# Weight pieces and expert pieces handled two at a time, and a new hand-written order for the first tiles

## The chip, the cores and the metric

The kernel runs on one core of one Trainium2 chip. The metric is the device time of one execution in microseconds (us), the median of several runs. The profile is of one such execution, taken by the hardware profiler.

## The reference, cut to what matters

Three stages follow one another. The first is a gated linear attention over 4 batches, 8 heads, 768 steps and head size 48; the second a feed-forward layer with a leaky ReLU; the third gives each token to one of 8 experts, at most 384 tokens to each.

```python
for t in range(S):                       # attention, f = sigmoid(f_logit)
    state = f[:, :, t, :, None] * state + einsum('bhd,bhde', k[:, :, t], v[:, :, t])
    y[:, :, t] = einsum('bhd,bhde->bhe', q[:, :, t], state)
x = y as [3072, 384]
h = x @ w_in                             # 384 -> 2048
x = maximum(0.01 * h, h) @ w_out         # 2048 -> 384
...                                      # token -> expert by the order of the logits, 384 tokens per expert
out[mask] = maximum(x[mask] @ w1[e], 0) @ w2[e]      # 8 experts, 384 -> 1024 -> 384
```

## The kernel before, in words

The 3072 tokens are 24 tiles of 128. Attention goes tile by tile in chunks; a tile takes the steps `f` (decay: exponentials and a sum on TensorE into `P`), `p` (the scaled `ks` and `qs`), `k` (transposed keys `kT`, copied to `kp`), `a` (scores `A`, masked into `am`), `y` (output, and the state's update `U`) and `x` (a DMA transpose of the result `ys` into `xT`). Three tiles make a group; group g then goes through the second stage's first product (`first`, 16 row blocks f of 128 hidden columns, 9 matmuls of 384 columns into `hp` for each block) and second product (`second`, `xp`). All products run as high and low float16 halves, three matmuls for one.

The weights come as float64 bit patterns in pairs of int32. A piece of `w_in` (one block f of 128 columns) is loaded, put together into float32 by three VectorE instructions (`as_f32`: `winu`), copied to its high half by ScalarE (`winh`) and its low half made by VectorE (`winl`); `w_out` likewise (`woutu`, `wo`). `first` and `second` take a block only after its piece has been emitted (`ready`). The first eight pieces of `w_in` land in tiles of the later `gh` and `gl` buffers (`win_e`), the rest in a ring with the tag `ws` (`win_s`, `wout_s`, `xw_s`).

The expert weights (`w1`, `w2`) are read from HBM in 64 pieces of 128x768 float32, split into a high half by ScalarE (`expert_high`) and a low half by VectorE (`expert_low`), and written back to HBM (`w1d`, `w2d`), from which the third stage fetches one expert's rows. This stream runs beside the second stage, one piece for every 21 large matmuls emitted.

A `Driver` with a clock of its own, advanced by the emitted large matmuls, decides when attention, weight pieces and stream are emitted; each engine executes its own queue in order. For the first tiles the order is written by hand: `START` is the list of steps (a letter, a tile or piece, one part each) and `LOADS` that of the loads on SP's queue; a load waits there behind those ahead of it. Every recorded operation carries line 85, so tile names tell them apart.

Of the kernel before, what the change touches and what calls it, by code (L numbers as in the profile page):

```python
# [9 lines left out]
F32 = mybir.dt.float32  # L10
# [51 lines left out]


LOADS = """
f:0 f:1 qk:0 f:2 v:0 f:3 qk:1 v:1 qk:2 f:4 w:0 f:5 qk:3 w:1 v:2 w:2 qk:4 x:0 v:3 qk:5 x:1 x:2 w:3 w:4 w:5 w:6 w:7 v:4 w:8 w:9 v:5 w:10
"""
START = """
z7 f0 f1 f0 f1 p0 f2 f3 p1 p0 a0 p1 a0 f2 k0 a0 f3 a1 k0 a1 y0 k1 a1 p2 p2 p3 y0 y0 w0 k2 k1 p3 a2 k2 a2 y1 y0 w1 a2 f4 y1 y1 y1 f4 p4 w2 k3 a3 k3 a3
p4 y2 a4 w1 f5 f5 a3 x0 y2 y2 w0 w2 a4 y2 y3 w1 x1 p5 a4 y3 p5 a5 w0 w2 a5 k4 y3 x2 k4 a5 w3
"""  # L70


# [20 lines left out]
def body(tc, qk, v, f_logit, w_in, w_out, w_gate, w1, w2, out):  # L93
# [6 lines left out]
    Dm = H * D  # L100
# [6 lines left out]
    GW = 384  # L107
    RT = 3
    NWD = 0
    WU = 4  # L110
    LEAD, PACE0, W0, FT, PB = 3, 1300.0, 1000.0, 8, 3

    with ExitStack() as ctx:
# [49 lines left out]
                XT[name, n] = t  # L163

        qkT = [apool.tile([128, 2, NP, 128], F32, name=f"qkT{i}") for i in range(3)]
        NPC = 16
        WIC = FF // NPC
        FPC = NF // NPC
        w_in_s, w_out_s, w_in_n = {}, {}, set()

        def load_win(i):
            if i in w_in_n:
                return
            w_in_n.add(i)
            if i < 8:
                if i % 4 == 0:
                    w_in_s["early"] = gpool.tile([128, 4, KT, WIC, 2], I32, name="win_e", tag=("gh", "gl")[i // 4])
                t = w_in_s["early"][:, i % 4]
            else:
                t = aw.tile([128, KT, WIC, 2], I32, name="win_s", tag="ws", bufs=3)  # L180
            SP.dma_start(t, ap(w_in, i * WIC * 2, [[2 * FF, 128], [256 * FF, KT], [2, WIC], [1, 2]]))
            w_in_s[i] = t

        def load_wout(i):
            t = aw.tile([128, FPC, Dm, 2], I32, name="wout_s", tag="ws", bufs=3)
            SP.dma_start(t, ap(w_out, i * FPC * 256 * Dm, [[2 * Dm, 128], [256 * Dm, FPC], [2, Dm], [1, 2]]))
            w_out_s[i] = t


# [71 lines left out]
            return u.bitcast(F32)  # L261

        def split_win(i):
            s = slice(i * WIC, (i + 1) * WIC)
            r = as_f32(w_in_s.pop(i), "win")
            yield
            copy(winh[:, :, s], r, SWI)
            yield
            DVE.scalar_tensor_tensor(winl[:, :, s], r, SWI, winh[:, :, s], op0=OP.mult, op1=OP.subtract)
# [3 lines left out]

        def split_wout(i):
            r = as_f32(w_out_s.pop(i), "wout")
            s = slice(i * FPC, (i + 1) * FPC)
            copy(wo[:, s, 0], r, SWO)
            DVE.scalar_tensor_tensor(wo[:, s, 1], r, SWO, wo[:, s, 0], op0=OP.mult, op1=OP.subtract)

# [63 lines left out]

        def load_expert(src, dst, scale, e, i):

            t = aw.tile([128, XW], F32, name="xw_s", tag="ws", bufs=3)
            x = SP.dma_start(t, src[e * 128:(e + 1) * 128, i * XW:(i + 1) * XW])
            if turned_at:
                behind(x, turned_at[-1])
            xw_s.append(t)  # L350

        def expert_high(src, dst, scale, e, i):
            x = xw_s.pop(0)
            o = aw.tile([128, XW], F16, name="xw_h", tag="wu", bufs=WU)
            z = copy(o, x, scale)
            if fed:
                behind(z, fed[-1][0])
            xw_o.append((dst[e * 128:(e + 1) * 128, 2 * i * XW:2 * (i + 1) * XW], x, scale, o))

        def expert_low():  # L360
            to, x, scale, h = xw_o.pop(0)
            o = aw.tile([128, XW], F16, name="xw_l", tag="wsc", bufs=WU)
            z = DVE.scalar_tensor_tensor(o, x, scale, h, op0=OP.mult, op1=OP.subtract)
            if fed:
                behind(z, fed[-1][1])
            return (to[:, :XW], h), (to[:, XW:], o)

        def expert_weights():
            ps = list(expert_pieces())
            for p in ps[:2]:  # L370
                load_expert(*p)

            n0 = big[0]
            for n in range(len(ps) + 1):
                while big[0] < n0 + n * PX:
                    yield 100.0
                if n < len(ps):
                    expert_high(*ps[n])
# [158 lines left out]
        def first(gi, nn, gx):  # L537
            xh, xl = gx[:, :KT], gx[:, KT:]
            N = 128 * nn
            gp = g2pool[0] if gi == LAST else gpool  # L540
            gh = gp.tile([128, NF, GW], F16, name="gh")
            gl = gp.tile([128, NF, GW], F16, name="gl")
            gh_[gi], gl_[gi] = gh, gl
            for f in range(NF):
                while ("in", f * NPC // NF) not in ready:
                    yield None
                fs = slice(128 * f, 128 * (f + 1))
                hp = psum.tile([128, GW], F32, name="hp", tag="mm", bufs=3)[:, :N]
                for c in range(KT):
                    mm(hp, winh[:, c, fs], xh[:, c, :N], c == 0, False)  # L550
                    yield N / 2.4
                    mm(hp, winh[:, c, fs], xl[:, c, :N], False, False)
                    yield N / 2.4
                    mm(hp, winl[:, c, fs], xh[:, c, :N], False, c == KT - 1)
                    if c < KT - 1:
                        yield N / 2.4
                a = SG / (SX * SWI)
                with tc.high_priority():
                    if f % 2 == 0:
                        g = work.tile([128, 2, GW], F32, name="g32")  # L560
                    t = g[:, f % 2, :N]
                    i = copy(t, hp, 0.01 * a)
                    fed.append((i, DVE.scalar_tensor_tensor(t, hp, a, t, op0=OP.mult, op1=OP.max)))
                    big[0] += 3 * KT
                    if f % 2:
                        s = slice(f - 1, f + 1)
                        copy(gh[:, s, :N], g[:, :, :N])
                        DVE.tensor_tensor(gl[:, s, :N], g[:, :, :N], gh[:, s, :N], op=OP.subtract)
                yield N / 2.4
# [5 lines left out]
        def second(gi, n, m):  # L575
# [2 lines left out]
            w = Dm  # L578
            xp = psum.tile([128, Dm], F32, name="xp", tag="mm", bufs=3)
            for f in range(NF):  # L580
                while ("out", f * NPC // NF) not in ready:
                    yield None
                mm(xp, gh[:, f, s], wo[:, f, 0], f == 0, False)
                yield w / 2.4
                mm(xp, gh[:, f, s], wo[:, f, 1], False, False)
                yield w / 2.4
                mm(xp, gl[:, f, s], wo[:, f, 0], False, f == NF - 1)
                big[0] += 3
                if f < NF - 1:
                    yield w / 2.4  # L590
# [499 lines left out]
        def go(key, n, parts=99):  # L1090
# [5 lines left out]
            for _ in range(parts):  # L1096
                try:
                    next(live[key, n])
                except StopIteration:
                    complete.add((key, n))  # L1100
                    if key == "x":
                        attended.add(n)
                    if key == "w":
                        ready.add(("in", n))
                    return

        def loads_after(n):
# [73 lines left out]

        def weights():
            yield W0
            for i in range(NPC):
                if ("w", i) in complete:
                    continue
                go("w", i)
                if i >= 8:
                    if i + 3 < NPC:
                        load_win(i + 3)  # L1190
                    else:
                        load_wout(i + 3 - NPC)
                yield WP
            tc.keep_in_program_order(DVE.tensor_scalar(wgs[:, :, 0], wg_s, SWG, None, op0=OP.mult))
            tc.keep_in_program_order(DVE.scalar_tensor_tensor(wgs[:, :, 1], wg_s, SWG, wgs[:, :, 0], op0=OP.mult, op1=OP.subtract))
            for i in range(NPC):
                split_wout(i)
                ready.add(("out", i))
                if i + 3 < NPC:
                    load_wout(i + 3)  # L1200
                yield 2300.0
            yield from expert_weights()
            ready.add("experts")

# [131 lines left out]
```

## Time and profile before

| | |
|---|---|
| median of 3 runs | 766.51 us (766.18 to 768.72) |
| the profiled execution's own time | 769.31 us |
| its span in the profile | 767.5 us, mean granted clock 0.988 |
| TensorE busy | 730.4 us of the span (95%) |
| VectorE busy | 553.3 us (72%) |
| ScalarE busy | 342.4 us (45%) |

Busy time is the time in which an engine has an instruction running; matmuls are pipelined, so that a busy TensorE is not one at its peak. The chain that ended last goes through TensorE for 54% of the span and through VectorE for 24%.

### The profile page before, as it was taken

To read this page: it belongs to the slowest core of one execution; us is meant where nothing else is said; L and a number is where in the kernel's file an instruction comes from. 1 tells how busy PE (TensorE), PEld (TensorE's weight loads), DVE (VectorE), ACT (ScalarE), POOL (GpSimd) and SP (SyncE) were. 2 spreads that over 40 slices of the span, in tenths; PEclk is the share of its full clock that TensorE was granted. 3 is DMA by queue.
4 is the path that set the end of the run, shared out by engine and by line. 5 is a ranking of instruction groups with operands and counts; after the bars stand their busy time and mean duration, and the time that the engine had idled before them with its cause. 6 is when DMAs were issued, how large, how long until landed. Compare 5 with 4: busy or idle time off the path is not lost.

```text
span 767.5 us, 15427 instructions
## 1 busy us (share of the span) xinstructions
PE 730.4 (95%) x5907; PEld 475.9 (62%) x5907; DVE 553.3 (72%) x1613; ACT 342.4 (45%) x714; POOL 94.4 (12%) x124
## 2 busy tenths in 40 slices
PE   8997999999999999999999999999989899999995
PEld 6773666676676677676666665555545456556663
DVE  7997999989848877867955758767677576772320
ACT  7676565567737656645744550000313123312320
POOL 3000000000000000000000001100443424535111
PEclk9998999999999999999999999999999999999998
DMA  9996445798987988998999100140674646774200
GB/s 242 210 225 200 132 137 167 195 274 243 272 241 200 293 239 213 258 270 191 254 264 231 63 1 12 42 165 32 220 191 146 205 125 158 232 217 167 94 32 31
DMA packets 111644, 135.91 MB, mean 177 GB/s; under 512 B 62929, under 2 KB 94674, under 8 KB 109522
## 3 DMA queue, kind: packets, MB, share of 16 engines
q1 hardware_dynamic: 106194, 100.31, 50.4%
q0 software_dynamic: 5376, 34.61, 13.3%
q8 instruction: 46, 0.75, 0.4%
q14 instruction: 28, 0.23, 0.1%
HBM read 86.52 MB, written 34.60 MB: 158 GB/s over the span
## 4 chain that ended last, share of the span: by engine, by line
PE 54%; DVE 24%; issue 8%; DMA 7%; ACT 4%; POOL 1%; SPq 0%; another core or an unknown queue 0%; POOLq 0%; ACTq 0%; DVEq 0%
PE hp L85 20%; PE xp L85 18%; PE yp L85 6%; DVE g L85 3%; PE y L85 3%; DVE gl L85 3%; DMA win_e<-in_moe_w_in 2%; DVE xw_l L85 2%; ACT gh L85 2%; PE c L85 1%; PE P L85 1%; DVE woutu L85 1%; DVE St L85 1%; DVE am L85 1%; DVE ahl L85 1%
## 5 line engine op out<-in xcount | busy, mean ns | idle before, releaser
L85 PE MATMUL hp<-xT,winh 128*128 128x384 f16 x768 | 191.5, 328 | 7.5 <-ACT winh L85 3.8
L85 PE MATMUL xp<-wo,gh 128*128 128x384 f16 x768 | 191.4, 326 | 2.4 <-ACT wo L85 1.2
L85 PE MATMUL hp<-xT,winl 128*128 128x384 f16 x384 | 126.1, 328 | 1.4 <-DVE winl L85 1.1
L85 PE MATMUL xp<-wo,gl 128*128 128x384 f16 x384 | 125.0, 326 | 0.0
L85 PEld LDWEIGHTS <-gh 128*128 128x128 f16 x912 | 83.7, 97 | 43.2 <-issue 0.9
L85 PEld LDWEIGHTS <-winh 128*128 128x128 f16 x768 | 73.0, 98 | 51.4 <-ACT winh L85 6.3
L85 PE MATMUL hp<-x2T,w1e 128*128 128x384 f16 x576 | 101.0, 329 | 0.8 <-ACT x2T L85 0.6
L85 PE MATMUL yp<-w2e,hh 128*128 128x384 f16 x384 | 95.5, 328 | 0.0
L85 ACT ACTIVATE g<-hp 128x384 f32<-128x384 f32 x152 | 73.0, 483 | 37.9 <-PE hp L85 35.3
L85 DVE SCALAR_TENSOR_TENSOR g<-hp,g 128x384 f32<-128x384 f32 x128 | 69.9, 552 | 11.5 <-ACT g L85 10.7
L85 DVE TENSOR_TENSOR gl<-g,gh 128x768 f16<-128x768 f32 x64 | 61.2, 956 | 19.2 <-ACT gh L85 18.8
L85 PEld LDWEIGHTS <-w1e 128*128 128x128 f16 x576 | 52.8, 98 | 33.7 <-issue 2.4
L85 ACT ACTIVATE gh<-g 128x768 f16<-128x768 f32 x64 | 53.8, 841 | 29.7 <-DVE g L85 29.4
L85 PEld LDWEIGHTS <-gl 128*128 128x128 f16 x528 | 48.8, 97 | 28.8 <-DVE gl L85 0.9
L85 ACT ACTIVATE xw_h<-xw_s 128x768 f16<-128x768 f32 x64 | 53.1, 839 | 24.4 <-DMA xw_s<-in_moe_w 16.4
L85 PE MATMUL yp<-w2e,hl 128*128 128x384 f16 x192 | 63.0, 328 | 0.0
L85 DVE SCALAR_TENSOR_TENSOR xw_l<-xw_s,xw_h 128x768 f16<-128x768 f32 x64 | 60.1, 950 | 0.6 <-ACT xw_h L85 0.6
L85 ACT ACTIVATE hh<-hp 128x384 f16<-128x384 f32 x64 | 31.4, 490 | 64.0 <-PE hp L85 52.7
L85 POOL IOTA jp<- 128x128 f32 x2 | 0.5, 238 | 454.2 <-PE hp L85 454.2
L85 ACT ACTIVATE x<-yp 128x384 f32<-128x384 f32 x24 | 11.8, 490 | 93.5 <-PE yp L85 75.4
L85 PEld LDWEIGHTS <-winl 128*128 128x128 f16 x384 | 37.8, 98 | 25.3 <-DVE winl L85 3.3
L85 ACT ACTIVATE x<-xp 128x384 f16<-128x384 f32 x24 | 11.7, 489 | 86.9 <-PE xp L85 76.2
(262 smaller groups left out, 1149.2 us busy)
## 6 DMA issues: line engine op xcount, KB each, us to landing
xw_s<-in_moe_w SPq DMA_DIRECT2D x64, 384.0 KB, 4.3
qkT<-in_qk SPq DMA_DIRECT2D x48, 192.0 KB, 4.9
wout_s<-in_moe_w_out SPq DMA_DIRECT2D x16, 384.0 KB, 3.3
w1d<-xw_h SPq DMA_DIRECT2D x32, 192.0 KB, 3.0
w1d<-xw_l SPq DMA_DIRECT2D x32, 192.0 KB, 4.9
w2d<-xw_h SPq DMA_DIRECT2D x32, 192.0 KB, 3.4
w2d<-xw_l SPq DMA_DIRECT2D x32, 192.0 KB, 4.3
fT<-in_f_logit SPq DMA_DIRECT2D x24, 192.0 KB, 3.8
```

What stands on the lines that cost most here:

```text
L85: i = f(*args, **kwargs)
```

## The change

`w_in` is cut into 8 pieces of one block and 4 of two, `w_out` into 8 of two. A double piece has one load, one set of three `as_f32` instructions, one high and one low copy, all twice as long, and its blocks become `ready` together. The ring `ws` holds two double tiles in place of three single ones. The expert stream loads two pieces with one DMA and writes both halves of a piece with one store, out of one tile of a ring of 3 (`wu`), where the halves had two rings of 4. `START` and `LOADS` are written anew.

```diff
 LOADS = """
-f:0 f:1 qk:0 f:2 v:0 f:3 qk:1 v:1 qk:2 f:4 w:0 f:5 qk:3 w:1 v:2 w:2 qk:4 x:0 v:3 qk:5 x:1 x:2 w:3 w:4 w:5 w:6 w:7 v:4 w:8 w:9 v:5 w:10
+f:0 f:1 qk:0 qk:1 f:2 w:0 v:0 f:3 qk:2 v:1 f:4 qk:3 f:5 w:1 w:2 qk:4 v:2 x:0 qk:5 v:3 x:1 x:2 w:3 w:4 w:5 w:6 w:7 v:4 w:8 w:9 v:5
 """
 START = """
-z7 f0 f1 f0 f1 p0 f2 f3 p1 p0 a0 p1 a0 f2 k0 a0 f3 a1 k0 a1 y0 k1 a1 p2 p2 p3 y0 y0 w0 k2 k1 p3 a2 k2 a2 y1 y0 w1 a2 f4 y1 y1 y1 f4 p4 w2 k3 a3 k3 a3
+z7 f0 f1 f0 p0 f1 p1 p0 p1 k0 a0 k0 k1 f2 a0 a1 a0 f3 w0 f2 p2 k1 y0 a1 p2 f3 a2 a1 k2 y0 y0 p3 a2 y0 a2 f4 p3 w0 k2 y1 x0 y1 w1 y1 y1 w1 k3 a3 f4 w0
...
-    WU = 4
+    WU = 3
...
+        IN = [(f, 1) for f in range(8)] + [(f, 2) for f in range(8, NF, 2)]
+        OUT = [(f, 2) for f in range(0, NF, 2)]
...
-                t = aw.tile([128, KT, WIC, 2], I32, name="win_s", tag="ws", bufs=3)
+                t = aw.tile([128, KT, 128 * n, 2], I32, name="win_s", tag="ws", bufs=2)
...
-            t = aw.tile([128, XW], F32, name="xw_s", tag="ws", bufs=3)
-            x = SP.dma_start(t, src[e * 128:(e + 1) * 128, i * XW:(i + 1) * XW])
+            t = aw.tile([128, 2 * XW], F32, name="xw_s", tag="ws", bufs=2)
+            x = SP.dma_start(t, src[e * 128:(e + 1) * 128, i * XW:(i + 2) * XW])
...
-            o = aw.tile([128, XW], F16, name="xw_h", tag="wu", bufs=WU)
-            z = copy(o, x, scale)
+            o = aw.tile([128, 2, XW], F16, name="xw_o", tag="wu", bufs=WU)
+            z = copy(o[:, 0], x, scale)
...
-                stores = expert_low() if n else ()
-                if n + 2 < len(ps):
+                store = expert_low() if n else ()
+                if n % 2 == 0 and n + 2 < len(ps):
                     load_expert(*ps[n + 2])
-                for x in stores:
-                    SP.dma_start(*x)
+                if store:
+                    SP.dma_start(*store)
...
-                    if i + 3 < NPC:
-                        load_win(i + 3)
+                    if i + 2 < len(IN):
+                        load_win(i + 2)
                     else:
-                        load_wout(i + 3 - NPC)
-                yield WP
+                        load_wout(i + 2 - len(IN))
+                yield n * WP
```

What this moves is seen best in the queues themselves. At the start of SP's queue the loads stood so before (`fT` is a tile's decay input, `qkT` its queries and keys in two DMAs, `ld_v` its values, `win_e` a piece of `w_in`):

```order
L85 DMA fT_99<-in_f_logit 128x384
L85 DMA qkT_85<-in_qk 48x1024 x2
L85 DMA fT_100<-in_f_logit 128x384
L85 DMA ld_v<-in_v 128x384
L85 DMA fT_98<-in_f_logit 128x384
L85 DMA qkT_86<-in_qk 48x1024 x2
```

and stand so now:

```order
L85 DMA fT_99<-in_f_logit 128x384
L85 DMA qkT_85<-in_qk 48x1024 x2
L85 DMA qkT_86<-in_qk 48x1024 x2
L85 DMA fT_100<-in_f_logit 128x384
L85 DMA win_e<-in_moe_w_in 128x3x256
L85 DMA ld_v<-in_v 128x384
L85 DMA fT_98<-in_f_logit 128x384
```

The second tile's queries and keys went ahead of three loads, and the first weight piece ahead of the first values.

VectorE's queue in the middle of group 0, around the blocks 8 to 10, before (`g` and `gl` are group 0's own activations, `winu` and `winl` the weight work):

```order
L85 SCALAR_TENSOR_TENSOR winl<-winu,winh 128x3x128
L85 SCALAR_TENSOR_TENSOR winu<-win_s,winu 128x384
L85 TENSOR_SCALAR winu<-win_s 128x384
L85 TENSOR_TENSOR gl<-g_706,gh 128x768
L85 SCALAR_TENSOR_TENSOR winl<-winu,winh 128x3x128
L85 SCALAR_TENSOR_TENSOR winu<-win_s,winu 128x384
L85 SCALAR_TENSOR_TENSOR g_741<-hp,g_741 128x384
L85 SCALAR_TENSOR_TENSOR winu<-win_s,winu 128x384
L85 TENSOR_SCALAR winu<-win_s 128x384
L85 SCALAR_TENSOR_TENSOR ys<-y,ys 128x384
L85 SCALAR_TENSOR_TENSOR winl<-winu,winh 128x3x128
```

and at the same blocks now:

```order
L85 SCALAR_TENSOR_TENSOR winu<-win_s,winu 128x768
L85 SCALAR_TENSOR_TENSOR g_687<-hp,g_687 128x384
L85 TENSOR_TENSOR gl<-g_650,gh 128x768
L85 SCALAR_TENSOR_TENSOR g_687<-hp,g_687 128x384
L85 SCALAR_TENSOR_TENSOR winu<-win_s,winu 128x768 x2
L85 TENSOR_TENSOR gl<-g_687,gh 128x768
L85 SCALAR_TENSOR_TENSOR winl<-winu,winh 128x3x256
L85 SCALAR_TENSOR_TENSOR winu<-win_s,winu 128x768
L85 SCALAR_TENSOR_TENSOR ys<-y,ys 128x384
L85 SCALAR_TENSOR_TENSOR St_113<-U,St_113 48x4x48 x2
L85 SCALAR_TENSOR_TENSOR winl<-winu,winh 128x3x256
```

Two blocks now become whole with one `winl`, and two `winl` end four blocks.

SP's queue in the middle of the expert stream, before (a load, and a store for each half):

```order
L85 DMA w2d<-xw_h 128x768
L85 DMA xw_s<-in_moe_w 128x768
L85 DMA w2d<-xw_l 128x768
L85 DMA xw_s<-in_moe_w 128x768
L85 DMA w2d<-xw_l 128x768
L85 DMA w2d<-xw_h 128x768
```

and now:

```order
L85 DMA w1d<-xw_o 128x1536
L85 DMA xw_s<-in_moe_w 128x1536
L85 DMA w1d<-xw_o 128x1536
L85 DMA w2d<-xw_o 128x1536
```

A load serves two pieces and a store both halves of one, so that two pieces take three entries where they took six.

## Rows read from the trace of the kernel before

**Rows 1.** The page's first part: busy time, share of the span, instructions.
```profile
PE 730.4 (95%) x5907; PEld 475.9 (62%) x5907; DVE 553.3 (72%) x1613; ACT 342.4 (45%) x714; POOL 94.4 (12%) x124
```

**Rows 2.** Windows: stretch, length, busy us (instructions) per engine, PEclk, DMA share, GB/s.
```profile
8.00:31.00 23.00, 22.34 (x224) 20.93 (x224) 19.45 (x37) 16.41 (x51) 0.00 (x0) 1.00 1.06 205
34.30:79.20 44.90, 38.92 (x247) 25.07 (x245) 39.68 (x86) 29.51 (x67) 0.00 (x0) 0.92 0.82 214
60.00:80.00 20.00, 14.87 (x75) 7.61 (x74) 16.52 (x37) 12.01 (x27) 0.00 (x0) 0.83 0.58 179
82.00:129.00 47.00, 46.33 (x357) 32.11 (x357) 45.91 (x93) 28.94 (x63) 0.00 (x0) 1.00 0.50 139
129.00:160.00 31.00, 29.23 (x261) 20.58 (x261) 28.97 (x61) 16.54 (x38) 0.00 (x0) 1.00 0.82 228
160.00:200.00 40.00, 37.31 (x312) 26.10 (x310) 37.45 (x65) 30.39 (x62) 0.00 (x0) 1.00 0.90 242
200.00:440.00 240.00, 237.92 (x2051) 160.92 (x2050) 175.72 (x316) 139.39 (x270) 0.00 (x0) 1.00 0.87 231
```

**Rows 3.** Timeline of TensorE at the end of group 0: start, us, instruction [idle before <-releaser].
```profile
64.28 0.50 PE L85 MATMUL hp<-xT,winh 128*128 128x384 f16 x2 [1.09 <-ACT winh L85]
67.78 0.50 PE L85 MATMUL hp<-xT,winh 128*128 128x384 f16 x2 [1.60 <-ACT winh L85]
69.04 0.34 PE L85 MATMUL hp<-xT,winl 128*128 128x384 f16 x1 [0.76 <-DVE winl L85]
78.29 0.91 PE L85 MATMUL y<-St,qs 128*128 128x96 f32 x6 [0.69 <-ACT kp L85]
81.96 0.48 PE L85 MATMUL hp<-xT,winh 128*128 128x384 f16 x2
```

**Rows 4.** VectorE: groups by line (busy, mean ns), and two places of its timeline.
```profile
L85 DVE SCALAR_TENSOR_TENSOR winu<-win_e,winu 128x384 int32<-128x384 int32 x16 | 8.7, 554 | 0.2
L85 DVE TENSOR_SCALAR winu<-win_e 128x384 int32<-128x384 int32 x8 | 2.8, 354 | 0.6 <-DMA win_e<-in_moe_w_in 0.6
L85 DVE SCALAR_TENSOR_TENSOR xw_l<-xw_s,xw_h 128x768 f16<-128x768 f32 x64 | 60.1, 950 | 0.6 <-ACT xw_h L85 0.6
44.78 1.02 DVE L85 SCALAR_TENSOR_TENSOR winu<-win_e,winu 128x384 int32<-128x384 int32 x2
78.68 0.56 DVE L85 SCALAR_TENSOR_TENSOR winl<-winu,winh 128x384 f16<-128x384 f32 x1
```

**Rows 5.** Timeline of the start: SP's queue, TensorE, VectorE, and group 0's first matmul.
```profile
4.81 0.80 SPq L85 DMA_DIRECT2D qkT<-in_qk  x2
7.91 1.16 PE L85 MATMUL A<-qs,ks 64*128 64x128 f32 x16 [1.32 <-DVE qs L85]
10.28 0.69 DVE L85 TENSOR_TENSOR ks<-qkT,ek 128x512 f32<-128x512 f32 x1 [2.42 <-DMA qkT<-in_qk]
31.02 0.34 PE L85 MATMUL hp<-xT,winh 128*128 128x384 f16 x1
```

**Rows 6.** The chain that ended last: start, us, what (two pieces of it).
```profile
205.41 1.09 PE A L85 x16
410.38 7.82 PE hp L85 x48
```

**Rows 7.** Timeline of TensorE where it waits for blocks of `w_out`.
```profile
129.22 0.32 PE L85 MATMUL xp<-wo,gh 128*128 128x384 f16 x1 [0.52 <-DVE wo L85]
141.85 0.32 PE L85 MATMUL xp<-wo,gh 128*128 128x384 f16 x1 [1.20 <-ACT wo L85]
```

**Rows 8.** DMA issues (KB each, us to landing), and ScalarE's timeline in the expert stream.
```profile
xw_s<-in_moe_w SPq DMA_DIRECT2D x64, 384.0 KB, 4.3
w1d<-xw_l SPq DMA_DIRECT2D x32, 192.0 KB, 4.9
261.21 0.84 ACT L85 ACTIVATE xw_h<-xw_s 128x768 f16<-128x768 f32 x1 [1.49 <-DMA xw_s<-in_moe_w]
264.35 0.84 ACT L85 ACTIVATE xw_h<-xw_s 128x768 f16<-128x768 f32 x1 [1.82 <-DMA xw_s<-in_moe_w]
```

More of the change, by code (lines that the diff above doesn't have):

```diff
@@ L64 @@
 LOADS = """
-f:0 f:1 qk:0 f:2 v:0 f:3 qk:1 v:1 qk:2 f:4 w:0 f:5 qk:3 w:1 v:2 w:2 qk:4 x:0 v:3 qk:5 x:1 x:2 w:3 w:4 w:5 w:6 w:7 v:4 w:8 w:9 v:5 w:10
+f:0 f:1 qk:0 qk:1 f:2 w:0 v:0 f:3 qk:2 v:1 f:4 qk:3 f:5 w:1 w:2 qk:4 v:2 x:0 qk:5 v:3 x:1 x:2 w:3 w:4 w:5 w:6 w:7 v:4 w:8 w:9 v:5
 """
 START = """
-z7 f0 f1 f0 f1 p0 f2 f3 p1 p0 a0 p1 a0 f2 k0 a0 f3 a1 k0 a1 y0 k1 a1 p2 p2 p3 y0 y0 w0 k2 k1 p3 a2 k2 a2 y1 y0 w1 a2 f4 y1 y1 y1 f4 p4 w2 k3 a3 k3 a3
-p4 y2 a4 w1 f5 f5 a3 x0 y2 y2 w0 w2 a4 y2 y3 w1 x1 p5 a4 y3 p5 a5 w0 w2 a5 k4 y3 x2 k4 a5 w3
+z7 f0 f1 f0 p0 f1 p1 p0 p1 k0 a0 k0 k1 f2 a0 a1 a0 f3 w0 f2 p2 k1 y0 a1 p2 f3 a2 a1 k2 y0 y0 p3 a2 y0 a2 f4 p3 w0 k2 y1 x0 y1 w1 y1 y1 w1 k3 a3 f4 w0
+a3 w2 p4 p4 x1 a3 f5 y2 k3 f5 a4 w2 y2 y2 y3 a4 p5 y3 a4 p5 w2 a5 x2 y3 k4 y2 a5 w1 a5 w3
 """
@@ L165, in body @@
         qkT = [apool.tile([128, 2, NP, 128], F32, name=f"qkT{i}") for i in range(3)]
-        NPC = 16
-        WIC = FF // NPC
-        FPC = NF // NPC
+        IN = [(f, 1) for f in range(8)] + [(f, 2) for f in range(8, NF, 2)]
+        OUT = [(f, 2) for f in range(0, NF, 2)]
         w_in_s, w_out_s, w_in_n = {}, {}, set()
@@ L174, in load_win @@
             w_in_n.add(i)
+            f, n = IN[i]
             if i < 8:
                 if i % 4 == 0:
-                    w_in_s["early"] = gpool.tile([128, 4, KT, WIC, 2], I32, name="win_e", tag=("gh", "gl")[i // 4])
+                    w_in_s["early"] = gpool.tile([128, 4, KT, 128, 2], I32, name="win_e", tag=("gh", "gl")[i // 4])
                 t = w_in_s["early"][:, i % 4]
             else:
-                t = aw.tile([128, KT, WIC, 2], I32, name="win_s", tag="ws", bufs=3)
-            SP.dma_start(t, ap(w_in, i * WIC * 2, [[2 * FF, 128], [256 * FF, KT], [2, WIC], [1, 2]]))
+                t = aw.tile([128, KT, 128 * n, 2], I32, name="win_s", tag="ws", bufs=2)
+            SP.dma_start(t, ap(w_in, f * 256, [[2 * FF, 128], [256 * FF, KT], [2, 128 * n], [1, 2]]))
             w_in_s[i] = t
         def load_wout(i):
-            t = aw.tile([128, FPC, Dm, 2], I32, name="wout_s", tag="ws", bufs=3)
-            SP.dma_start(t, ap(w_out, i * FPC * 256 * Dm, [[2 * Dm, 128], [256 * Dm, FPC], [2, Dm], [1, 2]]))
+            f, n = OUT[i]
+            t = aw.tile([128, n, Dm, 2], I32, name="wout_s", tag="ws", bufs=2)
+            SP.dma_start(t, ap(w_out, f * 256 * Dm, [[2 * Dm, 128], [256 * Dm, n], [2, Dm], [1, 2]]))
             w_out_s[i] = t
@@ L263, in split_win @@
         def split_win(i):
-            s = slice(i * WIC, (i + 1) * WIC)
+            f, n = IN[i]
+            s = slice(128 * f, 128 * (f + n))
             r = as_f32(w_in_s.pop(i), "win")
@@ L275, in split_wout @@
             r = as_f32(w_out_s.pop(i), "wout")
-            s = slice(i * FPC, (i + 1) * FPC)
+            s = slice(OUT[i][0], sum(OUT[i]))
             copy(wo[:, s, 0], r, SWO)
@@ L344, in load_expert @@
         def load_expert(src, dst, scale, e, i):
-            t = aw.tile([128, XW], F32, name="xw_s", tag="ws", bufs=3)
-            x = SP.dma_start(t, src[e * 128:(e + 1) * 128, i * XW:(i + 1) * XW])
+            t = aw.tile([128, 2 * XW], F32, name="xw_s", tag="ws", bufs=2)
+            x = SP.dma_start(t, src[e * 128:(e + 1) * 128, i * XW:(i + 2) * XW])
             if turned_at:
                 behind(x, turned_at[-1])
-            xw_s.append(t)
+            xw_s.extend((t[:, :XW], t[:, XW:]))
         def expert_high(src, dst, scale, e, i):
             x = xw_s.pop(0)
-            o = aw.tile([128, XW], F16, name="xw_h", tag="wu", bufs=WU)
-            z = copy(o, x, scale)
+            o = aw.tile([128, 2, XW], F16, name="xw_o", tag="wu", bufs=WU)
+            z = copy(o[:, 0], x, scale)
             if fed:
@@ L360, in expert_low @@
         def expert_low():
-            to, x, scale, h = xw_o.pop(0)
-            o = aw.tile([128, XW], F16, name="xw_l", tag="wsc", bufs=WU)
-            z = DVE.scalar_tensor_tensor(o, x, scale, h, op0=OP.mult, op1=OP.subtract)
+            to, x, scale, o = xw_o.pop(0)
+            z = DVE.scalar_tensor_tensor(o[:, 1], x, scale, o[:, 0], op0=OP.mult, op1=OP.subtract)
             if fed:
                 behind(z, fed[-1][1])
-            return (to[:, :XW], h), (to[:, XW:], o)
+            return to, o.rearrange("p a b -> p (a b)")
         def expert_weights():
             ps = list(expert_pieces())
-            for p in ps[:2]:
-                load_expert(*p)
+            load_expert(*ps[0])
             n0 = big[0]
@@ L544, in first @@
             for f in range(NF):
-                while ("in", f * NPC // NF) not in ready:
+                while ("in", f) not in ready:
                     yield None
@@ L580, in second @@
             for f in range(NF):
-                while ("out", f * NPC // NF) not in ready:
+                while ("out", f) not in ready:
                     yield None
@@ L1103, in go @@
                     if key == "w":
-                        ready.add(("in", n))
+                        ready.update(("in", IN[n][0] + j) for j in range(IN[n][1]))
                     return
@@ L1183, in weights @@
             yield W0
-            for i in range(NPC):
+            for i, (f, n) in enumerate(IN):
                 if ("w", i) in complete:
@@ L1188, in weights @@
                 if i >= 8:
-                    if i + 3 < NPC:
-                        load_win(i + 3)
-                    else:
-                        load_wout(i + 3 - NPC)
-                yield WP
+                    if i + 2 < len(IN):
+                        load_win(i + 2)
+                    else:
+                        load_wout(i + 2 - len(IN))
+                yield n * WP
             tc.keep_in_program_order(DVE.tensor_scalar(wgs[:, :, 0], wg_s, SWG, None, op0=OP.mult))
             tc.keep_in_program_order(DVE.scalar_tensor_tensor(wgs[:, :, 1], wg_s, SWG, wgs[:, :, 0], op0=OP.mult, op1=OP.subtract))
-            for i in range(NPC):
+            for i, (f, n) in enumerate(OUT):
                 split_wout(i)
[L1198 to L1201, printed above, removed]
+                ready.update(("out", f + j) for j in range(n))
+                if i + 2 < len(OUT):
+                    load_wout(i + 2)
+                yield n * 2300.0
             yield from expert_weights()
```

## Prediction

> **What bounds the kernel now.** I read the busy shares first. TensorE is busy for 730.4 of 767.5 us [rows 1], and the change leaves it the same matmuls, so all that can be won is time in which it waits or runs at the low clock. The windows show where that is: 0.66 us in 8 to 31, 5.13 us in 60 to 80, 0.67 in 82 to 129, 1.77 in 129 to 160, 2.69 in 160 to 200 and 2.08 in the 240 us after it [rows 2]. The 60 to 80 stretch also has a mean granted clock of 0.83, where the others but the one that contains it have 1.00: at two levels, 1.2 and 2.4 GHz, 17% of 20 us are lost, 3.4 us [rows 2]. So before 440 us some 13 us of waits and 3.4 us of clock are on the table, over half of both in one place: the end of group 0's first product.
>
> The timeline of that place shows TensorE waiting for `winh` and `winl` of single blocks, 1.09, 1.60 and 0.76 us, then for a `kp` copy, 0.69 us, and group 1's first block starting at 81.96 [rows 3]. The producer is VectorE: from 34.3, where group 0's activations join the weight work, to the end of the last `winl` at 79.24 [rows 4] it is busy 39.68 of 44.90 us [rows 2]. Up to there TensorE goes at VectorE's pace; from 82 to 129 both are full (46.33 and 45.91 of 47) [rows 2].
>
> **The change part by part.**
>
> *VectorE's instructions.* Each of the 12 double pieces drops four VectorE instructions, 48 in all. A 384-element one takes 554 ns, a 768-element one of the same kind 950 [rows 4], hence some 158 ns fixed and 1.03 ns an element, and a drop is worth up to 158 ns. But two that don't wait for each other take 1.02 us together [rows 4], not 1.11, so for such a pair only 0.07 us goes. Bounds: 24 x 0.07 = 1.7 us and 48 x 0.158 = 7.6 us over the kernel; the three of one `as_f32` do depend on each other, so I stand nearer the upper end where they follow each other directly, and nearer the lower where other work lies between.
> The Trainium skill (VectorE: DVE Perf Modes, "The DRAIN you can't avoid") says that the next instruction doesn't start until the pipe is empty. By that alone the saving would be the full 7.6 us; the 1.02 us row disagrees, and the row decides.
>
> *Start.* SP's DMA for the second `qkT` left at 4.81 [rows 5]. It waits there for the clearing of its tile, which the change doesn't move, so it leaves no earlier; but three loads (0.59 MB) no longer lie ahead of it. At 205 GB/s [rows 2] those took 2.9 us, and it landed at 10.28, where `ks` waited 2.42 us for it [rows 5]; now some 8.5. In exchange the third tile's `fT` leaves after it, at 5.6. TensorE gets the first transposed keys ahead of the first scores; those need `ks` alone, 0.6 us before `qs`, so its 1.32 us gap at 7.91 [rows 5] halves. Before group 0's first matmul it has the same blocks in both orders, and ran them with 0.66 us of idle. I take 1.2 us at the first `hp` (31.02 to 29.8); bounds 0 (the later values and weight piece make a new gap) and 2.0 (all idle goes).
>
> *End of group 0.* Counted in VectorE's queue from the second score mask (its end is the 34.3) to the last `winl`: before, 57 instructions of 384 elements at 554 ns, 7 of 768 at 950, 14 shifts at 354 [rows 4] and 2.6 us of small ones, 45.8 us by durations against 39.68 measured, a factor of 0.87 from overlap. Now 29 of 384, 18 of 768, 5 single shifts, 5 double ones (not in the trace: between 354 and 708, I take 560) and 2.2 us: 40.0, times 0.87 = 34.7 us. So 5.0 us less lies ahead of the last `winl`: 16 instructions are gone, and the last pair stands further forward, since two blocks come with one emission. The 5.2 us of VectorE idle in that stretch I leave at 3.2 to 5.2, as some of it came from TensorE's low clock. The last `winl` ends at 34.3 - 1.2 + 34.7 + 4.2 = 72.0. Behind it TensorE has the rest of blocks 14 and 15, 16 matmuls at 7.82 / 48 = 0.163 us, 2.6 us, attention blocks between them (half of an `A`, whose 16 take 1.09 [rows 6], with `kT`, state product, `U`, `P`; 3.8 us, an estimate from that row) and the `kp` wait of 0.69 [rows 3]: group 1 begins at 79.1. Before it was 81.96 with 0.9 us less attention ahead of it, so 82.9 is the like place: **3.8, I take 4.0 us won**, the start's 1.2 included. Bounds: 0.6, if the low clock comes again and costs the same 3.4, and 6.0.
> The pair also costs: blocks 8 and 10 are whole only when 9 and 11 are. By the same count the `winl` of 8 stands 2.9 us of VectorE work further back, that of 11 some 3.5 us further forward. TensorE will wait at 8 for 2 to 4 us, more than now, but VectorE isn't held by that, so the end of the stretch doesn't move.
>
> *`w_out`.* TensorE waits 0.52 and 1.20 us for late `wo` blocks [rows 7]. The last `wo` has some 9 us less VectorE work ahead of it now, six times the longer wait; both go: **1.7 us won** (bounds 0 and 1.8, all the idle of that stretch).
>
> *Expert stream.* VectorE and ScalarE do the same work. SP's entries fall from six to three for two pieces; SP isn't waited for. In 160 to 200 TensorE's 2.69 us of idle stand beside a VectorE that is busy 37.45 of 40 [rows 2]; with its backlog gone I take half, 1.3 us. Against that: the even piece waits for a load of twice the bytes. One of 384 KB takes 4.3 us [rows 8]; 768 KB isn't in the trace: not below 4.3, not above 8.6, I take 5.5, since packets and the queue's other traffic are part of the 4.3. ScalarE already waits 1.49 and 1.82 us for loads [rows 8], but TensorE has three `hp` banks ahead and lost only 2.08 us in 240 [rows 2]. I charge 1.0 us. **Net 0.3 won** (bounds -12, below, and 2.7).
>
> Sum: 4.0 + 1.7 + 0.3 = 6.0 us. The profiled execution took 769.31 us, 1.8 above its span and 2.8 above the median of 766.51; its span would become 761.5 and its time 763.3, and the median 760.5.
>
> **The rivals.**
> *The ring holds ScalarE (slower).* A high half may be written only when the store of three pieces earlier has landed; before, of four. In the stretches of first products a piece comes every 3.1 us (261.21 to 264.35 [rows 8]). The store of piece n-3 leaves after its low half, about 1.5 us into piece n-2, and has 4.7 us; stores of half the size take up to 4.9 [rows 8]. Before it had 7.8. If the full store takes about 6 us, each of some 27 such pieces holds ScalarE over 1 us, the activations queue behind it, and half of that reaches TensorE: 27 x 0.65 = 18 less the 6 won: 778; at 5.5 us it is 772. It decides from a landing of about 5.2 us. For it: the DMA share of 0.9 there [rows 2]. Against it: a wait for one piece eases the next.
> *The clock falls again.* The waits at 64 to 69 came ahead of the fall. New waits at blocks 8 and 12 are as long; the loss of 3.4 us comes back, and 2.6 us stay won: 764. The Trainium skill (TensorE: Matmul & The Clock Gate, "HAM oscillation") says that repeated waits put TensorE back to 1.2 GHz; the trace agrees with that at 60 to 80. By it, this is the case.
> *It does nothing that can be seen.* VectorE's time saved is taken by waits on ScalarE, which has the double copies (840 ns or so) in its own queue, and group 0 ends where it did; `w_out` alone is won: 765 to 767.
> *All idle goes.* No clock fall (3.4), the waits at 60 to 80 (5.1), `w_out` (1.7), half of the rest (2.5): 754.
>
> **How the numbers follow.** Forecast (758 to 762) 0.40, all idle 0.09, clock again 0.20, nothing 0.15, ring 0.16. A measurement here tells 0.3%, 2.3 us, from no change, so 764.2 parts faster from the same and 768.8 that from slower. Faster: 0.40 + 0.09 + 0.6 of the clock's 0.20 = 0.61; same: 0.15 + 0.08 = 0.23; slower 0.16. The range leaves out the ring's long end and half of the best case: 754.5 to 769.
>
> **What would show it.** Right: group 1's first `hp` near 79, the last `winl` near 72; longer waits at block 8; no wait for `wo` at 129 and 142; granted clock 1.00 in 60 to 80. Wrong: ScalarE idle before the high halves on the stores to `w1d` and `w2d`, with TensorE's busy share in 200 to 440 under 0.98; the first `hp` after 31; a low clock near 55 or 70.

## The result, and the profile after

The changed kernel takes 771.5 us (median of 21 runs, 767.3 to 775.6), the kernel before 765.75 beside it (21 runs): a ratio of 1.0078, 95% interval 1.0063 to 1.0094. It is 6 us slower; the forecast was 760.5, 5 to 6 us faster, and the range ended at 769. The spans of the two profiled executions, 770.9 and 767.5, differ by less, because the profile of before had a long third stage, which the change doesn't touch: from its first matmul (at 546.30) to the end 221.2 us, where the changed kernel has 215.9 and runs 1 to 12, 17 and 18 below have 214.1 to 215.9. So three pieces of the span are compared below: to the first matmul of the second product (`xp`), from there to the third stage's first (`x2T`), and the rest.

The windows of the changed kernel, with the columns of [rows 2]:

```profile
31.00:60.00 29.00, 22.83 (x134) 15.47 (x135) 22.43 (x43) 14.42 (x31) 0.00 (x0) 0.82 0.82 212
60.00:80.00 20.00, 18.11 (x122) 12.37 (x121) 17.42 (x29) 15.54 (x36) 0.00 (x0) 0.91 0.81 243
82.00:129.00 47.00, 43.30 (x320) 30.98 (x319) 45.30 (x76) 26.88 (x52) 0.00 (x0) 1.00 0.51 144
129.00:160.00 31.00, 30.12 (x286) 21.74 (x285) 29.47 (x55) 17.19 (x35) 0.00 (x0) 1.00 0.83 223
160.00:200.00 40.00, 38.81 (x336) 27.39 (x336) 35.47 (x62) 31.12 (x66) 0.00 (x0) 1.00 0.88 233
200.00:440.00 240.00, 234.50 (x1956) 157.27 (x1955) 174.20 (x312) 137.99 (x267) 0.00 (x0) 0.99 0.90 232
```

Against [rows 2] the waits in 129 to 160 and 160 to 200 shrank, from 1.77 to 0.88 us and from 2.69 to 1.19; the forecast had 1.7 and 1.3 us won there. But there is a new hole ahead of all this: in 31 to 60 TensorE now waits 6.2 us and has a mean granted clock of 0.82. And 200 to 440 has 5.5 us of waits where it had 2.08.

Of these 6.2 us, 3.96 are one gap. TensorE's timeline shows it:

```profile
44.16 0.33 PE L85 MATMUL hp<-xT,winl 128*128 128x384 f16 x1
48.45 2.08 PE L85 MATMUL P<-span,ld 128*128 128x128 f32 x8 [3.96 <-ACT ld L85]
50.32 0.85 PE L85 MATMUL hp<-xT,winh 128*128 128x384 f16 x2
54.39 0.49 PE L85 MATMUL hp<-xT,winh 128*128 128x384 f16 x2
```

The chain that ended last says what is behind `ld`:

```profile
30.61 6.78 DMA win_e<-in_moe_w_in
37.39 0.02 issue
37.41 9.80 DMA fT<-in_f_logit
47.20 0.02 issue
47.23 0.53 ACT fT L85
47.76 0.02 issue
47.78 0.62 ACT ld L85
48.41 0.04 issue
48.45 2.08 PE P L85 x8
```

A load of 192 KB, the decay input of the seventh tile, left at 37.41 and landed 9.80 us later, and the weight copy `winh` of the next block stood behind its two activations in ScalarE's queue, until 48.30. Behind the wait the same pair of matmuls takes 0.85 us, up to 53.2, where it takes 0.49 later: the low level of the clock. (The Trainium skill, TensorE: Matmul & The Clock Gate, "HAM oscillation", says that a wait for a DMA puts TensorE back to the low clock; this trace agrees.)

Why was that load late? SP's queue, before and now, around the third transpose `xT`:

```
before                                       now
20 qkT_87<-in_qk  x2                         18 qkT_87<-in_qk  x2
21 DMA_TRANSPOSE xT<-ys                      19 ld_v<-in_v
22 fT_98<-in_f_logit                         20 DMA_TRANSPOSE xT<-ys  x2
23 DMA_TRANSPOSE xT<-ys                      21 win_e<-in_moe_w_in  x5
24 win_e<-in_moe_w_in  x5                    22 ld_v<-in_v
25 ld_v<-in_v                                23 win_s<-in_moe_w_in  x2 (double)
                                             24 ld_v<-in_v
                                             25 wg_s<-in_moe_w_gate
                                             26 fT_98<-in_f_logit
```

Neither `LOADS` names this load. It is emitted after the written order has ended, and the builder puts it where it finds room: before, ahead of the third transpose; now behind ten more DMAs, 3.9 MB of weights and values. I showed and costed only the start of this queue.

In the expert stream the page's part on DMA issues, with the columns of [rows 8], has

```profile
xw_s<-in_moe_w SPq DMA_DIRECT2D x32, 768.0 KB, 5.6
w1d<-xw_o SPq DMA_DIRECT2D x32, 384.0 KB, 5.7
w2d<-xw_o SPq DMA_DIRECT2D x32, 384.0 KB, 5.9
```

so the load is as I took it (5.5) and the stores are above the 5.2 us from which the ring rival decides. The waits of ScalarE and TensorE in 165 to 440 us (us in total, times, longest):

```profile
ACT xw_o L85 <- DMA w2d<-xw_o: 17.1, 9, 4.2
ACT xw_o L85 <- DMA w1d<-xw_o: 9.0, 9, 2.4
PE pg L85 <- DMA turned<-wo: 4.4, 3, 1.9
PE hp L85 <- DVE g L85: 1.7, 3, 0.8
```

Before, the same list had one wait of ScalarE for a store, 1.5 us, and 14.9 for loads; TensorE's `hp` waited 2.6 us for `g`, and no `pg` for `turned` (the DMA transposes of `wo` from which the gate's columns are made).

### The profile page after: what moved, and what is told of

Same layout as the page of the kernel before. It is cut to its first block, busy times and chain, and to the rows that moved or that the text cites. A ratio compares the mean times of both kernels' runs of the same rounds, so it can differ in the third digit from the quotient of the medians.

```text
span 770.9 us, 15176 instructions
## 1 busy us (share of the span) xinstructions
PE 731.5 (95%) x5907; PEld 478.8 (62%) x5907; DVE 551.8 (72%) x1565; ACT 343.1 (45%) x702; POOL 94.8 (12%) x124
## 4 chain that ended last, share of the span: by engine, by line
PE 57%; DVE 18%; DMA 11%; issue 7%; ACT 4%; POOL 1%; SPq 0%; POOLq 0%; ACTq 0%; DVEq 0%
PE hp L85 24%; PE xp L85 16%; PE yp L85 6%; DMA fT<-in_f_logit 3%; PE y L85 3%; DMA turned<-x 2%; DMA turned<-wo 2%; DVE gl L85 2%; PE P L85 2%; DVE g L85 2%; PE A L85 1%; PE U L85 1%; DVE woutu L85 1%; PE c L85 1%; DMA w2d<-xw_o 1%
## 5 line engine op out<-in xcount | busy, mean ns | idle before, releaser
L85 PE MATMUL hp<-x2T,w1e 128*128 128x384 f16 x576 | 99.1, 325 | 0.7 <-ACT x2T L85 0.6
L85 ACT ACTIVATE g<-hp 128x384 f32<-128x384 f32 x152 | 73.2, 484 | 34.1 <-PE hp L85 32.5
L85 PEld LDWEIGHTS <-gl 128*128 128x128 f16 x528 | 48.7, 97 | 29.5 <-DVE gl L85 0.9
L85 ACT ACTIVATE xw_o<-xw_s 128x768 f16<-128x768 f32 x64 | 53.5, 840 | 28.1 <-DMA w2d<-xw_o 17.1
L85 DVE SCALAR_TENSOR_TENSOR xw_o<-xw_s,xw_o 128x768 f16<-128x768 f32 x64 | 60.5, 950 | 7.2 <-ACT xw_o L85 7.2
```

Of the source, the lines that this page charges most:

```text
L85: i = f(*args, **kwargs)
```

## Experiments

The theory: the order lost by the late load (A), the stream by its stores, and the double weights won. The rivals: the work behind group 0 has slack, so that the load costs little (B); or the double pieces themselves lose. Eighteen kernels, each timed in five rounds beside the kernel before; ratios are to it.

**1. The load put early.** In the changed kernel's `LOADS`:

```diff
-... x:0 qk:5 v:3 x:1 x:2 w:3 ...
+... x:0 qk:5 v:3 x:1 f:6 x:2 w:3 ...
```

> The changed kernel with one load added to its written load order: the decay input of the seventh tile (fT) now leaves between the second and third transposes, where it stood in the kernel before, ahead of five w_in pieces, two double ones and two of values. Theory A (the late load is the loss): in the profile of the changed kernel that load left at 37.41 us, landed 9.8 us later, and TensorE stood 3.96 us idle on `ld` at 48.45 with the low clock behind it; with the load early both go, group 1's first block starts near 84 instead of 89.9, and of the 7.1 us the kernel takes 3 to 6 less: 766 to 769. Theory B (the w_out stage has slack): the lead of 9.4 us lost at group 1 had come down to 2.9 at 240 us anyway, so the load costs at most these 2.9, and the time is 769 to 772, with the waits for `turned` near 346, 358 and 371 still there.

767.31 us, 1.0042 (1.0017 to 1.0066). The wait for `ld` is gone, and the window 31 to 60 has

```profile
31.00:60.00 29.00, 26.98 (x201) 19.76 (x201) 27.11 (x52) 19.26 (x42) 0.00 (x0) 1.00 0.94 255
```

The first `xp` comes at 116.36 instead of 122.39. Nearly half of the loss is gone (0.36 of 0.78%), as A says; the waits for `turned` (4.2 us) stay.

**2. The mirror.** The kernel before with `f:6` at the end of its `LOADS`.

> The mirror of the first run: the kernel before with the same load put at the end of its written load order, behind nine single pieces of w_in. Nothing else differs. Theory A: the load lands near 45, `ld` comes late for TensorE, a gap of 2 to 4 us and the low clock follow ahead of 60 us, and the time is 3 to 6 us above the kernel before (769 to 772). Theory B: a gap of that kind in group 0, but within 1.5 us of the kernel before at the end.

766.26 us, 1.0031 (1.0000 to 1.0061): between the two theories. The gap came (2.53 us for `ld` at 47.30, first `xp` at 121.44), but the profiled execution, 773.3 us, is the slowest of twelve, ten of which lie at 762 to 768. The others have no profile, so it is open whether the load was late in all of them.

**3. The old order with everything else changed**: `START` and `LOADS` of before (without `w:10`).

> The changed kernel with START and LOADS of the kernel before (less the load of an eleventh w_in piece, which no longer exists); double pieces and the double expert stream stay. If the new order alone makes the loss (A), group 0 gains from the double pieces as the prediction had it: group 1 near 79 to 81, and the time 762 to 766. If the double pieces or the expert stream cost (B, or the ring of 3), the time stays at 768 to 772 though `fT` is early.

764.80 us, 1.0005 (0.9978 to 1.0033). The new order was the whole excess over the kernel before; but what the double pieces should have won isn't there.

**4. Stores cut in two again** (changed kernel, same tiles).

```diff
-            return to, o.rearrange("p a b -> p (a b)")
+            return (to[:, :XW], o[:, 0]), (to[:, XW:], o[:, 1])
```

> The changed kernel with the one store of a piece's halves made two again (same tiles, same ring of 3, same loads). In the changed kernel's profile a full store takes 5.7 to 5.9 us to land and ScalarE waits 27.5 us for stores. If the size of a store sets that and what reaches TensorE (the ring rival), two stores of half the size land in 4 to 5 us, ScalarE's waits on stores fall under 15 us and the time by 2 to 4 us, to 767 to 769. If the depth of the ring sets it, or if these waits don't reach TensorE, time and waits stay: 770 to 773.

771.30 us, 1.0104 (1.0063 to 1.0146): nothing won. ScalarE still waits 21.9 us for stores in 165 to 440. The size of a store alone isn't it.

**5 to 8. One part at a time.** Run 5 is run 3 with the stream of before: two tiles of input and three of output, taken once and kept, are cut into three input slots and four of each output.

```diff
-            t = aw.tile([128, 2 * XW], F32, name="xw_s", tag="ws", bufs=2)
+            t = take("x")            # of three slots
...
-            o = aw.tile([128, 2, XW], F16, name="xw_o", tag="wu", bufs=WU)
+            o = take("h")            # of four slots; take("l") for the low half
```

> The kernel of the third run (old order, double weight pieces) with the expert stream of the kernel before: a load for one piece, a store for each half, three input slots and four for each output. Theory A (the double stream's long transfers make the transposes `turned` late, and that costs what the double w_out pieces win): TensorE's waits for `turned`, 4.1 us in the third run, fall under 1 us, group 3's last block to group 4's last of the stage no longer lose 3 to 5 us, and the time is 2 to 4 us under the kernel before. Theory B (the double weights win nothing; the third run is level for want of any effect): within 1.5 us of the kernel before.

757.91 us, 0.9909 (0.9881 to 0.9937): faster than both kernels. Run 6 has the double stream alone, apart from this: its single weight pieces lie in halves of kept tiles (run 16 tries such tiles by themselves, with one half more).

> The kernel before with the double expert stream alone: loads of two pieces, one store for both halves, a ring of three output tiles; weights in single pieces and old order. A: `turned` comes late (TensorE waits 3 to 5 us for it), ScalarE waits over 20 us for stores, and the time is 3 to 5 us above the kernel before. B: the same waits, but no time: within 1.5 us.

769.31 us, 1.0059 (1.0033 to 1.0084). TensorE waits 9.5 us for `g` ahead of `hp`, in ten places, 2.6 us before; for `turned` only 0.7, against my expectation. Run 7 is run 3 with two loads and two stores where there was one:

> The kernel of the third run with every DMA of the expert stream cut in two again (two loads behind each other into one double tile, two stores out of one), tiles and ring of three unchanged. If the size of a transfer makes the transposes late, the waits for `turned` fall under 1.5 us and the time comes near that of the double weights alone. If the short ring, and the loads that come two at a time, do it, waits of 3 us or more and the time of the third run stay.

763.16 us, 0.9991 (0.9966 to 1.0016), not told apart from run 3, and 5 us above run 5 on the same chip: neither the number nor the size of the DMAs is what costs, which leaves the loads in pairs and the short ring. Run 8 is the kernel before with the new `START` and `LOADS`:

> The kernel before with the new START and LOADS alone (the eleventh w_in load stays, at the end); weights and expert stream are single. The builder puts the seventh tile's `fT` behind nine single w_in pieces here too. A: the load lands some 8 us after it is issued at 37, TensorE waits 2 to 4 us for `ld` near 48 with the low clock behind it, and the time is 3 to 6 us above the kernel before. B (the order costs only with double pieces in the queue): within 2 us of it.

770.56 us, 1.0081 (1.0054 to 1.0108). With single pieces everywhere, TensorE waits

```profile
47.45 2.08 PE L85 MATMUL P<-span,ld 128*128 128x128 f32 x8 [4.79 <-ACT ld L85]
```

and its first `xp` is at 122.43, as in the changed kernel. So -0.9% (weights), +0.6% (stream) and +0.8% (order) are the parts; their sum, 0.5%, is somewhat under the 0.78% of the whole, since with double weights the stream costs 1.0% (run 3 against 5).

**9, 10, 13, 14, 17, 18. What in the double stream costs.** All have the old order and the double weights. Run 9 is run 5 with three slots for each output, run 10 with one store for both halves out of four slots, run 13 the same out of three, run 14 is run 9 with one load for two pieces, run 17 has the double loads and the full stores out of three, and run 18 is the kernel of run 3 again, beside 17.

```diff
-                ring["h"] = [t[:, 0] for t in o] + [h[:, 2 * XW:3 * XW]]
+                ring["h"] = [t[:, 0] for t in o]                              # 9
...
-            return (to[:, :XW], h), (to[:, XW:], o)
+            return ((to, o),)                                                 # 10, 13, 17
...
-                if n + 2 < len(ps):
+                if n % 2 == 0 and n + 2 < len(ps):                            # 14, 17
```

> The kernel of the fifth run (old order, double weights, single expert stream) with three slots instead of four for each of the stream's outputs; nothing else differs. Theory A (the depth of the ring is what the double stream lost): ScalarE waits 20 us or more for stores where the fifth run had 1.4, TensorE waits longer for hp banks behind g, and the time is 3 to 6 us above the fifth run: 761 to 764. Theory B (the size of the transfers lost it): ScalarE's waits for stores stay under 8 us and the time within 1.5 us of the fifth run: 757 to 760.

> The kernel of the fifth run with one store for both halves of a piece, out of a ring of four tiles for both halves; loads single. A (depth): ScalarE waits under 8 us for stores although each takes 5 to 6 us to land, and the time is within 1.5 us of the fifth run: 757 to 760. B (size): the long stores make the transposes `turned` late, TensorE's waits for them grow from 2.5 to 4 us or more, and the time is 2 to 5 us above the fifth run: 760 to 763.

> The kernel of the tenth run (old order, double weights, single loads, one store for both halves) with a ring of three tiles instead of four. A (full store and short ring together are the cost, as the ring rival of the prediction had it): ScalarE waits over 20 us for stores and the time is 4 to 7 us above the tenth run, 761 to 765. B (the double loads are the cost): under 10 us of such waits and 757 to 759.

> The kernel of the ninth run (old order, double weights, half stores from two rings of three) with one load for two pieces. A (the store and the ring are the cost): within 1.5 us of the ninth run, 756 to 759. B (the double loads are the cost): 761 to 765, with longer waits of TensorE for g or for turned.

> Old order, double weights, the full double stream (loads of two pieces, one store for both halves, ring of three), but its tiles taken once and kept instead of from a pool's ring. If double loads and the short ring with full stores together make the loss, this is level with the third run: a ratio to the kernel before of 0.998 to 1.003, ScalarE waiting over 20 us for stores. If the pool's ring makes the rest of it, 0.993 to 0.997.

> The kernel of the third run beside the seventeenth on the same chip, tiles from the pool's ring: 0.998 to 1.003 of the kernel before, as in the third run.

| run | loads | stores | slots | median us | ratio (interval) | ScalarE for stores / loads | TensorE (`hp` for `g`, `pg` for `turned`) | first `xp` to `x2T` |
|---|---|---|---|---|---|---|---|---|
| 5 | single | half | 4 | 757.91 | 0.9909 (0.9881 to 0.9937) | 1.4 / 16.8 | 0.6 / 2.5 | 427.6 |
| 9 | single | half | 3 | 757.32 | 0.9926 (0.9902 to 0.9950) | 0.3 / 15.4 | 0.5 / 1.2 | 426.1 |
| 10 | single | full | 4 | 757.37 | 0.9927 (0.9900 to 0.9953) | 0 / 26.8 | 0.7 / 0.4 | 426.2 |
| 13 | single | full | 3 | 763.59 | 0.9932 (0.9905 to 0.9959) | 28.2 / 0 | 0.2 / 1.5 | 425.5 |
| 14 | double | half | 3 | 766.05 | 0.9963 (0.9932 to 0.9994) | 2.7 / 12.3 | 1.9 / 2.5 | 429.0 |
| 17 | double | full | 3 | 764.16 | 1.0005 (0.9988 to 1.0022) | 28.4 / 0 | 3.2 / 5.3 | 434.5 |
| 18 | double | full | 3 | 765.24 | 1.0006 (0.9987 to 1.0026) | 29.5 / 0 | 3.8 / 5.2 | 435.1 |

The waits are those of 165 to 440 us. Runs 13 to 16 had a chip on which the kernel before takes 769.4 us; ratios are to be compared, not medians. Run 9 speaks against A (depth) and run 10 against B (size): neither the short ring nor the long store costs anything that can be seen by itself. Run 13 is the telling one:

```profile
ACT xw_o L85 <- DMA w2d<-xw_o: 15.2, 10, 2.4
ACT xw_o L85 <- DMA w1d<-xw_o: 13.0, 10, 3.0
PE pg L85 <- DMA turned<-wo: 1.5, 2, 0.8
PE hp L85 <- DVE g L85: 0.2, 1, 0.2
```

Both together hold ScalarE for 28 us, and TensorE sees nothing of it, against my expectation of 4 to 7 us. Now run 17, in which the loads come two at a time as well:

```profile
ACT xw_o L85 <- DMA w2d<-xw_o: 18.7, 10, 4.6
ACT xw_o L85 <- DMA w1d<-xw_o: 9.7, 9, 2.9
PE pg L85 <- DMA turned<-wo: 5.3, 3, 2.2
PE hp L85 <- DVE g L85: 3.2, 4, 1.7
```

The holds are as many and as much, but the longest is 4.6 us where it was 3.0, and TensorE waits 8.5 us where it waited 1.7. Double loads alone cost 0.3 to 0.4%: 0.9963 against 0.9926 of run 9, with intervals that overlap, and 766.05 against 763.59 us of run 13 on the same chip. With full stores and three slots they cost 0.7% (17 against 13). Runs 17 and 18 agree, so it doesn't matter that the changed kernel takes its tiles from a pool.

(The Trainium skill, DMA: Bandwidth & Descriptors, "Rules for kernel authors", asks for transfers of 1 MiB or more where the most bandwidth is wanted. The rate agrees: 768 KB land in 5.6 us, two loads of 384 KB in 4.3 each [rows 8]. But the time gains nothing by it: run 14 isn't faster than run 9.)

**11, 12, 16. Which weights won.** Run 11 has double pieces in `w_in` alone, run 12 in `w_out` alone, run 16 in neither; all three in kept tiles with four half tiles for the loads.

```diff
+        OUT = [(f, 2) for f in range(0, NF, 2)]      # 12; (f, 1) in 11 and 16
-                t = aw.tile([128, KT, WIC, 2], I32, name="win_s", tag="ws", bufs=3)
+                t = room("x", i, [KT, WIC, 2], 1)    # of four half tiles
```

> The kernel before, old order and single stream, with w_in in 8 single and 4 double pieces and w_out in 16 single ones. By the prediction's terms (4.0 us from group 0, 1.2 of them from the order) it would be 2.8 us under the kernel before, 760.5 to 762. By the traces of the third and fifth run, in which the first w_out block's work begins at 115.5 against 116.0 us, double w_in pieces win next to nothing: within 1.5 us of the kernel before, 762 to 765.

> The kernel before, old order and single stream, with w_out in 8 double pieces and w_in in 16 single ones. By the prediction's term it wins 1.7 us. By the traces of the fifth run, which is 2.7 us ahead at 336 matmuls of the first product and 6.4 us at 576, double w_out pieces carry most of the fifth run's 5.7 us: 758 to 760.

> The kernel before, single weight pieces, single stream, old order, with the weights and the stream in the persistent tiles of the eleventh and twelfth runs (four half tiles for the loads where a ring of three was). Nothing is double. If double pieces won the time in those runs, this one is level with the kernel before, 762 to 765; if the tiles did, it is at 758 to 761.

759.55 us, 0.9948 (0.9928 to 0.9967); 758.60, 0.9935 (0.9911 to 0.9958); 766.31, 0.9970 (0.9942 to 0.9997), on the slower chip. Either half wins most of what both do, `w_in` too, against what I expected; 0.3% of the 0.5 and 0.65% may belong to the deeper ring of the kept tiles. The two gains don't add up; one reason is shown below, at the end of group 0.

**15. Run 9 with the new order and `f:6` early.**

> The kernel of the ninth run with the new START and LOADS and the seventh tile's decay input early, as in the first run. If the late load is all that the new order costs, 756 to 759; if the order has a cost of its own, as the first run against the third says (0.37% between them), 759 to 762.

763.91 us, 0.9920 (0.9890 to 0.9951), against 0.9926 of run 9, and 763.59 us of run 13 on the same chip. By the medians nothing is left of the new order's cost. Two things speak for a rest. The profiled execution (765.01 us) has its first `hp` at 33.51 and its first `xp` at 119.11, 4.0 us behind run 13's. And runs 1 and 3, on one chip, are 2.5 us apart in their medians (0.37% by the ratios, with intervals that overlap). So the late load is a part of the order's cost, and whether it is all of it stays open.

## Why the prediction was wrong

**Start: the step that failed most.** I counted 1.2 us won at the first `hp` from three loads that no longer lie ahead of the second `qkT`, and looked no further down the queue. The second `ks` did begin earlier, at 8.84 instead of 10.28. But the third transpose left at 27.86, where it had left at 27.70, so the first `hp` came at 32.22, not 29.8, behind 1.25 us of waiting for that `xT`. And behind it lay the real cost, for which the sum has no term: the seventh `fT`, behind ten more DMAs. The new order alone costs 0.8%, 6 us the wrong way (run 8), and with the old order the changed kernel is level (run 3). The one load costs 0.3% in the old order (run 2), 0.36% in the changed kernel (run 1) and, by the medians of run 15, all of the 0.8%; its share stays open.

**End of group 0: right up to the last `winl`; then a wait that the sum doesn't have.** Run 5 has this part under the old order, so that without the start's 1.2 us the forecast is 73.2 for the last `winl` and 80.3 for group 1. The last `winl` ends at 73.2 (before 79.24 [rows 4]), and the last of group 0's 144 matmuls begins at 75.57 (before at 80.53). TensorE's waits there:

```profile
64.91 1.46 PE L85 MATMUL hp<-xT,winh 128*128 128x384 f16 x4 [3.17 <-ACT winh L85]
78.43 1.13 PE L85 MATMUL y<-St,qs 128*128 128x96 f32 x8 [1.30 <-ACT kp L85]
83.07 0.48 PE L85 MATMUL hp<-xT,winh 128*128 128x384 f16 x2 [0.44 <-DMA xT<-ys]
```

The pair's wait is 3.17 us, within the 2 to 4 that I gave it, and the low clock follows it again (mean granted clock 0.83 in 60 to 80, as before): the rival "the clock falls again" happened here, and still the `winl` ended when the forecast had it. But group 1 begins at 83.07, since its third tile wasn't ready. ScalarE wrote that tile's high half at 55.48; VectorE came to the low half only at 78.80, behind the last `winl`, two `gl` and the first work on `w_out` (three `woutu`), and the transpose left behind that:

```profile
55.48 0.49 ACT L85 ACTIVATE ys<-y 128x384 f16<-128x384 f32 x1 [1.00 <-PE y L85]
78.80 0.55 DVE L85 SCALAR_TENSOR_TENSOR ys<-y,ys 128x384 f16<-128x384 f32 x1
79.38 1.24 SPq L85 DMA_TRANSPOSE xT<-ys  x1
```

Run 11 has the same double pieces of `w_in`, but single ones of `w_out`. It has the same wait of 3.17 us, but there `ys` stands right behind the last `winl` (at 71.43), and group 1 begins 6 us earlier:

```profile
72.38 0.55 DVE L85 SCALAR_TENSOR_TENSOR ys<-y,ys 128x384 f16<-128x384 f32 x1
77.01 0.49 PE L85 MATMUL hp<-xT,winh 128*128 128x384 f16 x2
```

The first `xp` is at 115.52 in run 5 and at 111.95 in run 11, against 116.03 before: 0.5 and 4.1 us won, where the sum had 2.8 beside the start. So the step that failed is that group 1 begins when the last `winl` and TensorE's own blocks are done; the sum has no term for `ys` and its transpose. (These are single executions, and no run moves `ys` alone.)

**VectorE.** Its busy time fell by 3.0 us in run 5 (553.3 to 550.3), inside the bounds of 1.7 and 7.6 but nearer the lower one. A double shift takes 550 to 559 ns; I took 560. (I set the 1.02 us row against the Trainium skill, VectorE: DVE Perf Modes, "The DRAIN you can't avoid". That section goes on to say that a next instruction which is not held starts earlier, and the row fits that.)

**`w_out` and its neighbour: right.** I had 1.7 us in 129 to 160 and 1.3 in 160 to 200. Run 5 waits 0.87 and 0.32 us there, against 1.77 and 2.69: 3.3 us won, near the 3.0 of the sum. (The 9 us that I put beside the longer wait are 7.5 times it, not six.) From the first `xp` to `x2T` it is 2.7 us ahead of before. Together with group 0 that is 3.2 us of the 5.7 to 7 that the medians give; in which stretch of other executions the rest lies stays open.

**Expert stream: the sign wrong.** I charged 1.0 us for coarser loads against 1.3 won. It costs 0.6% by itself and 1.0% with double weights (runs 6; 5 against 3). The load's landing was right (5.6 against 5.5). The ring rival named the place and the threshold: stores land in 5.7 to 5.9 us, above 5.2, and ScalarE is held 19 times for 27.5 us over the kernel (I had 27 pieces). But its price went by "half of that reaches TensorE", and run 13 shows that none of it does so long as pieces arrive one at a time: TensorE waits 1.7 us there, as it does in run 9, where ScalarE is held 0.3 us. For the cost it takes loads of two pieces too. I had the two in separate terms and never together. Why bunched pieces make the holds longer, and what share of the cost is `turned` landing late, was argued from the waits and not tried apart.

**What was to show it wrong** did: first `hp` after 31, the low clock near 50 and again at 74 to 77, ScalarE idle on the stores to `w1d` and `w2d`, and TensorE's share in 200 to 440 at 0.977, under 0.98.

## What to carry to other kernels

Where a scheduler places what the written order doesn't name, compare the whole queue before and after, not the part that was edited: here one 192 KB load that went behind ten others kept TensorE waiting for 4 us, and the new order with it cost as much as the double weights won. Ask of the next stage not only when its weights are ready but when its input is. Cost a coarser stream with its buffers, stores and loads together; here the short ring and the full store were free, alone and together, the double loads cost 0.3 to 0.4%, and all three 0.8 to 1.0%. Time the parts apart before giving up on a change: double weight pieces with the old order and single stream take 757.3 to 757.9 us, 0.7 to 0.9% under the kernel before.

## What was not expected of the hardware

A load of 192 KB, which takes 4.5 us as the median of its kind in this kernel, took 9.80 us behind 3.9 MB of weights and values on the same queue, although the queue had issued it. And ScalarE's holds of up to 3.0 us in run 13, 28 us of them in 275, didn't reach TensorE: it waited 1.7 us there, and 1.7 in run 9 without them.
